# An S4 convolution block with its gradients: the Y tables of the dK reduction made beside their use, and one column tile's transform moved ahead of the K transform

## The chip, the core and the metric

The kernel runs on one core of a Trainium2 chip. The metric is device time in microseconds (us) of one execution; lower is better. Several executions are timed and the median is given. One execution was recorded by the hardware profiler.

The engines that matter here: PE (TensorE, matmuls and transposes), DVE (VectorE, elementwise), ACT (ScalarE, copies and activations), POOL (GpSimd; here almost only an issuer of DMAs) and SP (an issuer of DMAs). Each engine runs its own instructions strictly in the order in which they were written. POOL's and SP's queues, too, issue DMAs in that order, so a DMA that must wait for a buffer holds those behind it.

## The reference

Length L = 2048, width D = 512, state N = 128 per channel, FFN width F = 1792. Everything is bf16 at the boundary.

```python
x  = A_u                              # [1, 2048, 512]
xn = layernorm(x)
dt = exp(log_dt); dB = dt * B; logdA = dt * A          # complex, [512, 128]
K[d, l] = Re( sum_n C[d,n] * dB[d,n] * exp(logdA[d,n] * l) )
s  = causal_long_convolution(xn, K) + Dskip * xn       # along the sequence, FFT in the reference
g  = silu( silu(xn @ w1) @ w2 )
out = x + s * g
# outputs: out, and the vjp with grad_out for A_u, A_re, A_im, B_re, B_im, C_re, C_im,
#          log_dt, Dskip, w1, w2
```

The kernel replaces the FFT by matmuls with DFT tables. Its four "column tiles" `kt` = 0..3 are blocks of frequencies. For each it needs three spectra: U of `xn`, DS of the gradient that enters the convolution, and K. It stores them as UXd, DXd and KXd in DRAM (1 MB per tile). The products are U x K (the forward convolution y), conj(U) x DS (the gradient dK of K) and conj(K) x DS (the gradient for xn).

## The kernel before

All work is laid out by hand: `manual_schedule` keeps the order in which the Python program emits it, generators interleave several streams, and tiles come from two stacks of pools (left and right). Waits follow from the use of tiles. The program is five functions after each other.

**stage_1 (0 to 178 us)**: the FFN forward, the DFT tables, and the power tables XYd in DRAM: for each of `NB` = 4 blocks of channels a row of powers of exp(logdA), some of them times C dB.

**stage_2, table stage (178 to 302 us).** K at lag h*16 + l is a product of a high power (table X, 41 chunk positions h) and a low power times C dB (table CY, l = 0..15). `chunk_tables` (L795 to L845) builds X and CY on DVE: `prod` fills X from a few loaded powers (L819 to L823), `quads` fills the 12 missing low columns of a table (L806 to L813, 5 instructions). It also builds Y, the low powers without C dB, which only the backward pass needs; Y's low three columns serve as multipliers for CY too. `copy_tables` (ACT, L781) copies loaded base columns into Y and CY. `chunk_K` multiplies CY by X (PE); after block 3 `store_K` writes K's lags to DRAM and `load_K` reads them back in the order of the transform (K_b). In the same 15 steps per block, `gen_xt` transposes X (PE L932, ACT copy L934) and stores it as XTd, and `gen_yt` does so with Y (PE L950, ACT L951) as YTd, both on SP's queue; `fwd_classes` (L990, PE L998, ACT L999) transforms the column tiles of xn "by classes", 32 matmuls in 4 groups, leaving a radix-4 step (`rad4`, DVE L92 to L98) to finish; tile 3 of DS is done in the same way. While K travels through DRAM (the K wait), DVE does the last radix steps, the last Y quads, and the product conj(U) x DS of tile 3 (`cplx_mul`, L106 to L109) with its inverse radix step `rad_inv` into BK3.

**stage_3 (302 to 350 us), gen_kt**: four transforms of K (`fwd_eo` L1164, `add_eo` L1174 to L1179), the product with U, and the inverse radix step into BY. The rest of the XT and YT groups of block 3 is emitted between these steps.

**stage_4 (350 to 424 us)**: `DXform` transforms tiles 0, 1 and 2 of DS by the longer way, `fwd_eo` with 64 matmuls (`front`), then `mul` (add_eo and conj(U) x DS) and `inv` (into BK). Between them the y convolution runs on PE in steps `t0` of two (L1188, ps_v from BY): its result S_s (ACT L1442) is multiplied by cG = grad_out times a silu derivative of the loaded `co` (POOL loads L1323, ACT L132, DVE L1335 and L1340).

**stage_5 (424 to 575 us)** starts with the dK convolution (L1188 with BK) and, beside it on DVE, `Prod`: for each tile conj(K) x DS from KXd and DXd (loads aXl L1558) and the inverse step into BG. The DS spectrum of tile 2 is handed to Prod in SBUF. It goes on with the w2 gradient (PE L1594) and, from about 480 us, the **slab stage**: the convolution over BG (L1188), and `Slabs`, which reduces dK against the powers. Sixteen slabs (4 per block), each in three steps that a fixed grid deals out between convolution steps and halves of w2 groups (8 matmuls each):

- step 1: `P2(i, 0)`, 16 small matmuls (L1769) of a block-diagonal tile `Gbd` by the loaded XTl, with an ACT copy into Vb (L1771); `Gb(i+1)` on DVE (L1757);
- step 2: `P2(i, 1)`; `load(i+3)` (XTl on SP and POOL L1746, YTl on POOL L1747);
- step 3: `D3(i)` on DVE (L1780, L1783), Vb by YTl; then `P3(i-1)` on PE (L1798), the sum over l.

The grid for each w2 group `ft` from 4 is: one convolution step while any is left (ft up to 9), one slab step, half a group, two slab steps, half a group, two slab steps.

**stage_6 (575 to 752 us)**: the FFN backward and LayerNorm's gradient.

Of the kernel before, what the change touches and what calls it, by code (L numbers as in the profile page):

```python
# [135 lines left out]
def kernel(ctx, tc, A_u, A_A_re, A_A_im, A_B_re, A_B_im, A_C_re, A_C_im, A_log_dt, A_Dskip, B_x, B_w1, B_w2, grad_out,  # L136
# [28 lines left out]
    k.XTd = dr.tile([NB, 64 * NR, 2, P], BF16, name="XTd"); k.YTd = dr.tile([16, P, 2, 4, P], BF16, name="YTd")  # L165
# [121 lines left out]
class Setup:  # L287


    def __init__(self, k, W1, W2, pr, fs):  # L290
# [27 lines left out]
        k.num = const.tile([P, 49], I32, name="num")  # L318
# [403 lines left out]
def tables_open(k, fs):  # L722

    lo = k.left
    k.mm = lo.open("mm")
    sa = lo.open("sa")
    k.tabs, k.gt, k.gc = {}, {}, {}
    k.slot = [(sa, sa), None]
    XY = fs.tile([P, 11, 2, 64, 2], BF16, name="XYc", tag="aT")

    def more():
        k.nc.gpsimd.dma_start(XY[:].rearrange("p i c q e -> p i (c q e)"), k.XYd[:, 17:NT, 0])
# [4 lines left out]
    k.gt[0] = chunk_tables(k, 0)  # L737
    k.nt0 = 0
    k.ko = lo.open("ko"); k.xc = lo.open("xc")
    k.Kout = k.ko.tile([P, NH, P], BF16, name="Kout")  # L740


def ld_tab(k, b):

    XY = k.xc.tile([P, 11, 2, 64, 2], BF16, name="XYc", tag="XYc")
    k.nc.sync.dma_start(XY[:].rearrange("p i c q e -> p i (c q e)"), k.XYd[:, 17:NT, b])
    k.gc[b] = copy_tables(k, b, XY)
    k.gt[b] = chunk_tables(k, b)
# [13 lines left out]
def open_y(k, b):  # L762

    slot, cys = k.slot[b % 2]
    k.tabs[b]["Y"] = slot.tile([P, 2, 64, 16, 2], BF16, name="Y", tag="Y")
    k.tabs[b]["CY"] = cys.tile([P, 2, 64, 16, 2], BF16, name="CY", tag="CY")
# [13 lines left out]

def copy_tables(k, b, XY):  # L781

    Y, CY = k.tabs[b]["Y"], k.tabs[b]["CY"]

    def cp(x, o, i, n):
        k.nc.scalar.copy(out=cq(x, o), in_=XY[:, i:i + n].rearrange("p i c q e -> p (c q) i e"))
    cp(Y, slice(1, 4), 0, 3)
    yield
    cp(Y, slice(0, 16, 4), 3, 4)
    yield  # L790
    cp(CY, slice(0, 16, 4), 7, 4)
    yield


def chunk_tables(k, b):  # L795
# [6 lines left out]
    def quads(x, op0, op1):  # L802
        fl = lambda m: m.rearrange("p c q (a b) e -> p (c q) a b e", a=4)
        m1, m2 = mt("m1", 12), mt("m2", 12)
        qd = x[:].rearrange("p c q (a b) e -> p c q a b e", a=4)
        TT(out=fl(m1), in0=qd.rearrange("p c q a b e -> p (c q) a b e")[:, :, :, 0:1].to_broadcast([P, 128, 4, 3, 2]),  # L806
           in1=cq(t["Y"], slice(1, 4)).unsqueeze(2).to_broadcast([P, 128, 4, 3, 2]), op=ALU.mult)
        q4 = lambda m, c: m[:, c].rearrange("p q (a b) e -> p q a b e", a=4)
        for c in range(2):
            TT(out=q4(m2, c), in0=qd[:, c, :, :, 0:1].to_broadcast([P, 64, 4, 3, 2]), in1=t["Y"][:, 1 - c, :, 1:4].unsqueeze(2).to_broadcast([P, 64, 4, 3, 2]), op=ALU.mult)  # L810
        TT(out=qd[:, 0, :, :, 1:4], in0=q4(m1, 0), in1=q4(m1, 1), op=op0)
        i, j = (0, 1) if op1 == ALU.add else (1, 0)
        TT(out=qd[:, 1, :, :, 1:4], in0=q4(m2, i), in1=q4(m2, j), op=op1)  # L813
# [18 lines left out]
    if b == 0:  # L832
        quads(t["CY"], ALU.add, ALU.subtract)
        yield
# [6 lines left out]
    if b:  # L841
        quads(t["CY"], ALU.add, ALU.subtract)
        yield
    quads(t["Y"], ALU.subtract, ALU.add)
    yield  # L845
# [75 lines left out]
def gen_xt(k, xs, b):  # L921
# [3 lines left out]
    for n in range(11):  # L925
        ks = range(4 * n, min(4 * n + 4, 41))
        if n % 2 == 0:
            XT = xs.tile([P, 8, 2, P], BF16, name="XT", tag="XT", bufs=4)
# [9 lines left out]
        yield  # L938


def gen_yt(k, xs, i0):
    nc = k.nc
    YT = xs.tile([P, 2, 2, 4, P], BF16, name="YT", tag="XT", bufs=4)
    for i in (i0, i0 + 1):
        b, u, s, q0 = slab(i)
        Y = k.tabs[b]["Y"]
        pt = k.ps.tile([P, 2, 4, P], BF16, name="pt_yt", tag="ps")
        for c in range(2):
            for b4 in range(4):
                nc.tensor.transpose(out=pt[:, c, b4, :], in_=Y[:, c, q0 + 4 * b4:q0 + 4 * b4 + 4].rearrange("p w l e -> p (w l e)"), identity=k.ident[:])  # L950
        nc.scalar.copy(out=YT[:, i - i0], in_=pt[:])  # L951
        if i > i0:
            k.put(k.YTd[i0:i0 + 2].rearrange("i p c b n -> p i (c b n)"), YT[:].rearrange("p i c b n -> p i (c b n)"))
        yield
# [48 lines left out]
def stage_2(k):  # L1003
# [3 lines left out]
    k.tf2 = ro.open("tf2"); k.xs = ro.open("xs", 2); sb = ro.open("sb"); k.slot[1] = (sb, ro.open("cyb")); dsc = ro.open("dsc"); uw = ro.open("uw", 2)  # L1007
# [20 lines left out]
    for b in range(2):  # L1028
# [8 lines left out]
        for _ in fr:  # L1037
            tables_0(k)
    for b in range(NB):
# [3 lines left out]
        gy = [gen_yt(k, k.xs, i) for i in (4 * b, 4 * b + 2)]  # L1043
        sl = [gx] * 11 + [g for g in gy for _ in range(2)]
# [4 lines left out]
        if b == 2:  # L1049
            sl, gy2 = sl[:11], sl[11:]  # L1050
        if b:
            open_y(k, b + 1)
        fr = front(b + 2) if b < 2 else fwd_classes(k, dsc, k.DS, st["TF"], st.setdefault("D", {}))
        for j in range(15):
            if j in ((3, 9), (0, 3, 6), (0, 3))[b]:
                next(gw)
            if j in ((8, 10, 12, 14), (1, 4, 7, 10), (8, 13))[b]:
                next(fr)
            if j < 4:
                next(Tc, None)  # L1060
            if j == 0 and b < 2:
                next(k.gt[b])
# [15 lines left out]
    next(k.gt[2])  # L1078
    for g in gy2:
        next(g)  # L1080
# [8 lines left out]
    k.by = lo.open("by"); k.uxp = lo.open("uxl")  # L1089
    k.TFs1 = ld_tf(k, 1, nc.gpsimd)  # L1090
    UX = ld_ux(k, 0)
    radix(3)
    next(k.gt[3])
    sl = iter(sl)
    for n in range(8):
        next(next(sl))
# [5 lines left out]
    k.BY = k.by.tile([P, 4, 2, 4, W], BF16, name="BY", tag="B")  # L1102
    k.tn = lo.open("tn"); bk3 = lo.open("bk3")
    kq = k.kq = lo.open("kq")
    k.sel = lo.open("sel")
    k.row = k.sel.tile([DK, P], BF16, name="row")
# [6 lines left out]
    k.BK3 = rad_inv(k, bk3, "BK3", PX)  # L1113
    k.dskb = dskip_out(k)
    return gk, sl, held


def rad_inv(k, pool, tag, PX):

    B_ = pool.tile([P, 2, 4, W], BF16, name="BK", tag=tag)  # L1120
    t = k.mm.tile([P, 2, 4, W], BF16, name="r4_t", tag="cm_t2")
    rad4(k.nc, B_[:, :, 0:2], B_[:, :, 2:4], PX, t[:].rearrange("p e (c m) w -> p e c m w", c=2), True)
    return B_
# [143 lines left out]
def stage_3(k, gk, sl, held):  # L1267
# [3 lines left out]
    for n, _ in enumerate(gk, 1):  # L1271
# [4 lines left out]
        for g in (next(sl, None) for _ in range(n >= 4)):  # L1276
            if g is not None:
                next(g)
# [94 lines left out]
class DXform:  # L1373
# [7 lines left out]
    def front(self, kt):  # L1381
# [8 lines left out]
        for n, _ in enumerate(fwd_eo(k, A, lambda t: k.DS[:, t, :], TFs, TN)):  # L1390
            if n == 0 and kt < 2:
                k.TFs = ld_tf(k, kt + 1, k.nc.scalar)
            yield

    def mul(self, kt):
# [3 lines left out]
        if kt < 2:  # L1399
            nc.gpsimd.dma_start(k.DXd[kt], XD[:])  # L1400
        else:
            k.pr = Prod(k, XD)
        self.PX = cplx_mul(nc, k.mm, self.UX, XD, conj_a=True)
        if kt < 2:
            self.UX = ld_ux(k, kt + 1)

    def inv(self, kt):
        k = self.k
        k.BK.append(rad_inv(k, self.bk if kt else k.tf2, f"BK{kt}" if kt else "TFs", self.PX))
        if kt == 2:  # L1410
            k.BK.append(k.BK3)


def stage_4(k):
# [5 lines left out]
    k.bk = lo.open("bk")  # L1420
# [6 lines left out]
    for t0 in range(0, T, TS):  # L1427
# [3 lines left out]
        if t0 == 8:  # L1431
            for _ in dx.front(2):
                pass
            dx.mul(2)
# [18 lines left out]
        if t0 == 10:  # L1453
            dx.inv(2)
# [92 lines left out]
class Prod:  # L1547
# [4 lines left out]
    def __init__(self, k, XD):  # L1552
        self.k = k
        self.ld = {0: (self.get(k.kq, "A", k.KXd, 0), XD)}
# [49 lines left out]
def stage_5(k):  # L1604
# [40 lines left out]
    gs(T - 2)  # L1645
    Gt = k.Gt = k.tf2.tile([P, 16, 256], BF16, name="Gt", tag="TFs")
# [16 lines left out]
    lo.close("bk", "sel", "kq", "bk3", "tn", "uxl")  # L1663
# [52 lines left out]

class Slabs:
# [3 lines left out]
    def __init__(self, k, sw):  # L1721
# [5 lines left out]
        self.newV(0)  # L1727

# [9 lines left out]
    def load(self, i, q=None):  # L1738
        k, nc = self.k, self.k.nc
        dma = (q or nc.sync).dma_start  # L1740
        YT = self.YT[i] = self.sw.tile([P, 2, 4, P], BF16, name="YTl", tag="YT", bufs=4)
# [5 lines left out]
        nc.gpsimd.dma_start(YT[:], k.YTd[i])  # L1747
# [61 lines left out]
    def steps(self):  # L1809

        self.Gb(0)
        for i in range(16):
            self.P2(i, 0)
            if i + 1 < 16:
                self.Gb(i + 1)
            yield
            self.P2(i, 1)
            self.XT.pop(i), self.G.pop(i)
            if i + 3 < 16:
                self.load(i + 3)  # L1820
            yield
            self.D3(i)
            if i:
                self.P3(i - 1)
            if i > 1 and i % 4 == 1:
# [7 lines left out]
class Bwd:  # L1833
# [23 lines left out]
    def dh(self, n):  # L1857
# [5 lines left out]
        sd = self.fw.tile([P, 2, 512], BF16, name="sd", tag="sd")  # L1863
# [37 lines left out]
    def dx(self, tc_, dhT):  # L1901
# [3 lines left out]
        for t in range(4 * tc_, 4 * tc_ + 4):  # L1905
# [5 lines left out]
            dxn = k.fx.tile([P, D], F32, name="dxn", tag="dxn")  # L1911
            m12 = fw.tile([P, 2], F32, name="m12", tag="m12"); c12 = fw.tile([P, 2], F32, name="c12", tag="c12")
            nc.vector.scalar_tensor_tensor(out=dxn[:], in0=psx[:], scalar=1.0, in1=self.DXC[:, t, :], op0=ALU.mult, op1=ALU.add, accum_out=m12[:, 0:1])
            t1 = k.fx.tile([P, D], F32, name="ln_t1", tag="ln_t1", bufs=1)
            nc.vector.scalar_tensor_tensor(out=t1[:], in0=dxn[:], scalar=1.0, in1=k.xn[:, t, :], op0=ALU.mult, op1=ALU.mult, accum_out=m12[:, 1:2])
            nc.vector.tensor_scalar(out=c12[:], in0=m12[:], scalar1=k.rstd[:, t:t + 1], scalar2=-1.0 / D, op0=ALU.mult, op1=ALU.mult)  # L1916
            nc.scalar.activation(out=dxn[:], in_=dxn[:], func=ACT.Identity, scale=k.rstd[:, t:t + 1], bias=c12[:, 0:1])  # L1917
# [4 lines left out]
    def rest(self):  # L1922
# [7 lines left out]
        nc.vector.scalar_tensor_tensor(out=dxn[:], in0=k.xn[:, t, :], scalar=c12[:, 1:2], in1=dxn[:], op0=ALU.mult, op1=ALU.add)  # L1930
        O1 = fw.tile([P, D], BF16, name="O1", tag="O1")
# [110 lines left out]
```

## Time and profile before

| | us |
|---|---|
| three runs, median | 758.52 |
| three runs, lowest and highest | 752.28, 761.05 |
| the profiled execution, its own time | 754.35 |
| the profiled execution, its span | 752.2 |
| mean granted TensorE clock | 0.967 of full |
| PE busy | 665.2 (88%) |
| DVE busy | 619.8 (82%) |
| ACT busy | 444.4 (59%) |
| POOL busy | 124.4 (17%) |
| bytes moved by DMA | 198.86 MB, mean 264 GB/s |

All times of single instructions count from the start of the profiled span; 2 us of the execution's own time lie outside the span. An engine's busy time is summed over its instructions; PE's matmuls are pipelined, so that the recorded 0.38 us of a 512-wide matmul overlaps the next one, which starts 0.216 us later. An arrow after an idle time names what released the engine. A line number is that of the source; where a helper such as `rad4` or `cplx_mul` emits the instruction, all its callers share that line, and the name of the written tile tells them apart.

### The profile page before, as it was taken

Reading aid. Unit: us, or ns where it says so; the run is one execution under the profiler, and the core shown is the slowest. Engines: PE = TensorE matmul, PEld = TensorE weight load, DVE = VectorE, ACT = ScalarE, POOL = GpSimd, SP = SyncE. Lnnn points to the kernel's source line nnn. Section 1 sums busy time; section 2 is a strip of 40 time slices with the busy share of each in tenths; the row PEclk is TensorE's granted clock in tenths of the full one; section 3 lists DMA queues with packets and bytes.
Section 4 is the critical chain, followed back from the end, with each engine's and each line's share of the span. In section 5 each row is a group of like instructions: output and inputs, shape, how many; then the busy total and the mean of one; then the engine's idle time right before and its main releaser. Section 6 shows DMA issues by size and latency. Waiting matters only on the chain. (4 is left out here: it accounts for less than half of the span.)

```text
span 752.2 us, 13787 instructions
## 1 busy us (share of the span) xinstructions
PE 665.2 (88%) x5356; PEld 347.0 (46%) x5356; DVE 619.8 (82%) x965; ACT 444.4 (59%) x541; POOL 124.4 (17%) x192
## 2 busy tenths in 40 slices
PE   4768978798978777999999899989999999889998
PEld 2434444353646566454444344434444554444444
DVE  6899999998999798699999999654685579988810
ACT  4789888986769857375435322244566765764211
POOL 2334071021002003000012111311131000111210
PEclk9999998999989997999999999999999999999999
DMA  9647766899898969899667889798895987788591
GB/s 270 235 160 254 239 212 240 273 315 362 266 318 280 289 189 215 302 375 380 247 248 250 298 324 339 227 331 303 279 298 170 283 230 225 234 251 280 186 344 52
DMA packets 153155, 198.86 MB, mean 264 GB/s; under 512 B 29405, under 2 KB 114788, under 8 KB 147170
## 3 DMA queue, kind: packets, MB, share of 16 engines
q1 hardware_dynamic: 133314, 129.48, 54.6%
q0 software_dynamic: 11840, 54.07, 20.0%
q10 hardware_dynamic: 7936, 14.43, 5.9%
q8 instruction: 42, 0.69, 0.4%
q14 instruction: 23, 0.19, 0.1%
HBM read 112.72 MB, written 83.38 MB: 261 GB/s over the span
## 5 line engine op out<-in xcount | busy, mean ns | idle before, releaser
L607 PE MATMUL ps_h<-XNT,W 128*128 128x512 bf16 x224 | 61.1, 423 | 13.8 <-ACT hs L610 13.8
L1188 PEld LDWEIGHTS <-TIs 128*128 128x128 bf16 x384 | 37.3, 98 | 50.4 <-issue 4.4
L580 PE MATMUL ps_o<-W,aT 128*128 128x512 bf16 x224 | 54.3, 391 | 1.8 <-DVE ak L76 1.8
L1869 PE MATMUL ps_da<-DOT,W2T 128*128 128x512 bf16 x224 | 52.9, 379 | 1.5 <-ACT DOT L1849 1.1
L1908 PE MATMUL ps_dx<-W1T,dhT 128*128 128x512 bf16 x224 | 52.9, 379 | 0.0
L1870 DVE TENSOR_TENSOR dhT<-ps_da,sd 128x1024 bf16<-128x1024 f32 x28 | 34.1, 1221 | 22.0 <-ACT sd L132 16.3
L1594 PE MATMUL ps_w<-DO_all,AW 128*128 128x512 bf16 x224 | 52.0, 380 | 0.0
L1992 PE MATMUL ps_w<-dhc,xn 128*128 128x448 bf16 x256 | 49.3, 352 | 1.0 <-DMA dhc<-dhd 1.0
L1780 DVE TENSOR_TENSOR T<-Vb,YTl 128x2048 bf16<-128x2048 bf16 x16 | 19.6, 1223 | 35.9 <-ACT Vb L1771 35.6
L1164 PEld LDWEIGHTS <-TFs 128*128 128x128 bf16 x312 | 30.2, 98 | 37.4 <-issue 2.8
L934 ACT COPY XT<-pt_xt 128x1024 bf16<-128x1024 bf16 (+1 forms) x44 | 41.3, 1004 | 4.0 <-DMA XTd<-XT 3.0
L1771 ACT CAST Vb<-ps_V 128x1024 bf16<-128x1024 f32 x32 | 31.7, 1013 | 17.9 <-PE ps_V L1769 12.0
L607 PEld LDWEIGHTS <-W 128*128 128x128 bf16 x224 | 22.7, 105 | 39.4 <-issue 22.8
L1164 PE MATMUL ps_f<-K_b,TFs 128*128 128x512 bf16 x168 | 38.9, 379 | 1.7 <-DMA K_b<-Kud 1.2
L1917 ACT ACTIVATE dxn<-dxn,c,rstd 128x512 f32<-128x512 f32 x16 | 13.0, 814 | 45.0 <-DVE c L1916 45.0
L580 PEld LDWEIGHTS <-aT 128*128 128x128 bf16 x224 | 22.8, 102 | 31.2 <-issue 7.4
L1992 PEld LDWEIGHTS <-xn 128*128 128x128 bf16 x256 | 25.0, 98 | 24.9 <-DMA dhc<-dhd 1.5
L998 PE MATMUL ps_f<-xn,TFs 128*128 128x512 bf16 x128 | 33.1, 414 | 2.4 <-DMA TFs<-TFd 2.4
L1893 ACT COPY dhk<-pt_dh 128x1024 bf16<-128x1024 bf16 x28 | 28.0, 1001 | 10.2 <-PE pt_dh L1891 10.2
L1869 PEld LDWEIGHTS <-W2T 128*128 128x128 bf16 x224 | 21.6, 98 | 26.8 <-issue 2.2
L1164 PE MATMUL ps_f<-DS,TFs 128*128 128x512 bf16 x144 | 33.0, 379 | 0.7 <-ACT S_s L1442 0.7
L1594 PEld LDWEIGHTS <-AW 128*128 128x128 bf16 x224 | 20.2, 98 | 26.7 <-issue 4.7
(345 smaller groups left out, 1570.6 us busy)
## 6 DMA issues: line engine op xcount, KB each, us to landing
TIs<-TId SPq DMA_DIRECT2D x24, 512.0 KB, 6.5
XTd<-XT SPq DMA_DIRECT2D x20, 512.0 KB, 4.5
XTl<-XTd SPq DMA_DIRECT2D x15, 512.0 KB, 8.1
hTd<-hs SPq DMA_DIRECT2D x28, 256.0 KB, 3.5
akd<-ak SPq DMA_DIRECT2D x28, 256.0 KB, 3.6
UXl<-UXd POOLq DMA_DIRECT2D x7, 1024.0 KB, 7.9
dhd<-dhk SPq DMA_DIRECT2D x28, 256.0 KB, 5.3
XYd<-XYg SPq DMA_DIRECT2D x25, 256.0 KB, 4.5
```

Of the source, the lines that this page charges most:

```text
L580: nc.tensor.matmul(out=pso[:], lhsT=aT[:, ft, tt * P:(tt + 1) * P], rhs=W2[:, ft, :], start=(ft == 0), stop=(ft == FT - 1))
L607: nc.tensor.matmul(out=ps[:, j], lhsT=W1[:, dk, ft * P:(ft + 1) * P], rhs=XNT[:, dk], start=(dk == 0), stop=(dk == DK - 1))
L934: nc.scalar.copy(out=XT[:, j0:j0 + len(ks)], in_=pt[:, 0:len(ks)])
L998: nc.tensor.matmul(out=ps[:, c, :], lhsT=TFs[:, t1 + 4 * j, c, :], rhs=src[:, t1 + 4 * j, :], start=(j == 0), stop=(j == 3))
L1164: nc.tensor.matmul(out=ps[:, c, :], lhsT=tab(j), rhs=at(t1 + 4 * j), start=(n == 0), stop=(n == 4 * len(terms) - 1))
L1188: nc.tensor.matmul(out=ps[:, j, :], lhsT=TIs[:, j, 2 * kt + c, :], rhs=B[kt][:, c, (t0 + j) % 4, :], start=(kt == 0 and c == 0), stop=(kt ...
L1594: nc.tensor.matmul(out=ps[:], lhsT=A[:, t, :], rhs=k.DO[:, t, :], start=(t == 0), stop=(t == T - 1))
L1771: nc.scalar.copy(out=self.V[i][:, g2], in_=ps[:].rearrange("p b c n -> p c b n"))
L1869: nc.tensor.matmul(out=ps[:, j], lhsT=self.W2T[:, ft // 2, dk, j * P:(j + 1) * P], rhs=self.DOT[tc_][:, dk], start=(dk == 0), stop=(dk == ...
L1870: nc.vector.tensor_tensor(out=self.dhT[:, f0:f0 + 2, :], in0=ps[:], in1=sd[:], op=ALU.mult)
L1908: nc.tensor.matmul(out=psx[:], lhsT=dhT[:, ft, t % 4 * P:(t % 4 + 1) * P], rhs=self.W1T[:, ft, :], start=(ft == 0), stop=(ft == FT - 1))
L1992: nc.tensor.matmul(out=ps[:], lhsT=k.xn[:, t, dk * P:(dk + 1) * P], rhs=ch[i][:, t, :], start=(t == 0), stop=(t == T - 1))
```

## The change

**Y.** The Y tables, their transposes and YTd are no longer made in the table stage. What stays there is Yb, the low three columns (128x768) that CY's quads need. In the slab stage Y is built for half a block at a time, two slabs, numbered m = 0..7: `load_y` (two POOL loads per block) brings the seven base columns of Y from XYd; `Ybase(m)` copies them on ACT into the working tile Ys (and the low three into Yb for an even m); `Yquad(m, c)` fills the missing columns of component c with three DVE products of 128x768; `Yt(i)` transposes one slab's part with 8 PE transposes and an ACT copy into YT (two buffers), which D3 reads in the place of YTl.

```diff
+    def Yquad(self, m, c):
+        if m >= 8:
+            return
+        ...
+        for j in range(2):
+            TT(out=m4(j), in0=qd[:, j, :, :, 0:1].to_broadcast([P, 32, 4, 3, 2]),
+               in1=self.Yb[:, j ^ c, q0:q0 + 32].unsqueeze(2).to_broadcast([P, 32, 4, 3, 2]), op=ALU.mult)
+        TT(out=qd[:, c, :, :, 1:4], in0=m4(0), in1=m4(1), op=ALU.add if c else ALU.subtract)
+
+    def Yt(self, i):
+        k, nc = self.k, self.k.nc
+        pt = k.ps.tile([P, 2, 4, P], BF16, name="pt_yt", tag="ps")
+        for c in range(2):
+            for b4 in range(4):
+                q = 16 * (i % 2) + 4 * b4
+                nc.tensor.transpose(out=pt[:, c, b4, :], in_=self.Ys[:, c, q:q + 4].rearrange("p w l e -> p (w l e)"), identity=k.ident[:])
+        YT = self.YT[i] = self.sw.tile([P, 2, 4, P], BF16, name="YT", tag="YT", bufs=2)
+        nc.scalar.copy(out=YT[:], in_=pt[:])
 
     def steps(self):
         self.Gb(0)
         for i in range(16):
+            m = i // 2 + 1
             self.P2(i, 0)
             if i + 1 < 16:
                 self.Gb(i + 1)
+            if i % 2 == 0:
+                self.Yt(i)
             yield
             self.P2(i, 1)
             self.XT.pop(i), self.G.pop(i)
             if i + 3 < 16:
                 self.load(i + 3)
+            if i % 2 == 0:
+                self.Yt(i + 1)
             yield
             self.D3(i)
             if i:
                 self.P3(i - 1)
+            if i % 2 == 0:
+                self.Ybase(m)
+                if i % 4 == 0 and i < 12:
+                    load_y(k, i // 4 + 1)
+            self.Yquad(m, i % 2)
             if i > 1 and i % 4 == 1:
                 self.store(i // 4 - 1)
             yield
```

`Slabs.__init__` makes Y of pair 0 (`Ybase(0)`, `Yquad(0, 0)`, `Yquad(0, 1)`). In the table stage `quads(t["Y"], ...)`, `gen_yt` and their steps go, and the load of base columns is 7 columns in two DMAs instead of 11 in one:

```diff
-    quads(t["Y"], ALU.subtract, ALU.add)
-    yield
...
-        nc.gpsimd.dma_start(YT[:], k.YTd[i])
...
+def load_y(k, b):
+    for o, i, n in ((2048, 20, 4), (3072, 17, 3)):
+        k.nc.gpsimd.dma_start(k.yb[:, o:o + 256 * n].rearrange("p (i z) -> p i z", i=n), k.XYd[:, i:i + n, b])
```

**Tile 2 of DS.** It is transformed by classes in the table stage like tile 3 (32 matmuls), its radix step and the store DXd[2] come after `store_K`, and its product and inverse step run in place during the K wait. In stage 4 `front(2)`, `mul(2)` and `inv(2)` go, and Prod reads tile 2 of DS from DRAM, on POOL's queue ahead of the loads of `co` and `cG` for step 12:

```diff
-            if j in ((8, 10, 12, 14), (1, 4, 7, 10), (8, 13))[b]:
+            if j in ((6, 8, 10, 12, 14), (1, 4, 7, 10, 13), (2, 5, 8, 11))[b]:
                 next(fr)
...
     store_K(k)
-    next(k.gt[2])
-    for g in gy2:
-        next(g)
+    XD2 = st["D2"]["A"]
+    rad(XD2)
+    nc.gpsimd.dma_start(k.DXd[2], XD2[:])
...
     XD = st["D"]["A"]
     rad(XD)
     nc.gpsimd.dma_start(k.DXd[3], XD[:])
+    PX = cplx_mul(nc, k.mm, st[2]["A"], XD2, conj_a=True)
+    k.BK2 = XD2
+    rad_inv(k, XD2, PX)
     PX = cplx_mul(nc, k.mm, st[3]["A"], XD, conj_a=True)
...
         if t0 == 8:
-            for _ in dx.front(2):
-                pass
-            dx.mul(2)
+            k.pr = Prod(k)
...
-            dx.inv(2)
...
-        self.ld = {0: (self.get(k.kq, "A", k.KXd, 0), XD)}
+        self.ld = {0: (self.get(k.kq, "A", k.KXd, 0), self.get(k.kq, "X", k.DXd, 0))}
```

**Places.** The transform of U that stage 3 needs first is read into BY[:, 0] instead of a buffer of its own; XT has six buffers instead of four, and all XT groups of block 3 are emitted in the K wait, so that stage 3 holds none; some pools open earlier or later; in stage 6 the f32 rows `dxn` and `ln_t1` lie in one tile (`fx`) in the buffer of DS tile 2, still with two rows for `dxn`:

```diff
-            XT = xs.tile([P, 8, 2, P], BF16, name="XT", tag="XT", bufs=4)
+            XT = xs.tile([P, 8, 2, P], BF16, name="XT", tag="XT", bufs=6)
...
-    UX = ld_ux(k, 0)
+    UX = k.BY[:, 0]
+    nc.gpsimd.dma_start(UX, k.UXd[0])
...
-            dxn = k.fx.tile([P, D], F32, name="dxn", tag="dxn")
+            dxn = k.fx[:, t % 2]
```

More of the change, by code (lines that the diff above doesn't have):

```diff
@@ L832, in chunk_tables @@
     if b == 0:
-        quads(t["CY"], ALU.add, ALU.subtract)
+        quads()
         yield
@@ L937, in gen_xt @@
             k.put(k.XTd[b, P * k0:P * k1].rearrange("(k p) c n -> p k c n", p=P), XT[:, 0:k1 - k0])
[L938 to L953, printed above, removed]
         yield
```

184 lines of the change are left out of this document (103 added, 81 removed).

## The prediction

> **What bounds the kernel now.** I read the page first, then busy times by stage, then the chain of waits and the order of time inside the three places that the change touches.
>
> ```profile
> span 752.2 us, 13787 instructions
> PE 665.2 (88%) x5356; PEld 347.0 (46%) x5356; DVE 619.8 (82%) x965; ACT 444.4 (59%) x541; POOL 124.4 (17%) x192
> ```
>
> PE and DVE are both nearly full; the answer differs by stage. In the next view each row is a stretch in us, its length, then the busy time of PE, PEld, DVE, ACT and POOL, the granted clock and the DMA share.
>
> ```profile
> 178.00:240.00 62.00, 51.45 (x776) 31.83 (x778) 58.98 (x93) 42.94 (x48) 9.31 (x15) 0.92 0.92 301
> 240.00:302.00 62.00, 47.85 (x949) 37.10 (x942) 55.77 (x78) 45.95 (x53) 10.57 (x20) 0.89 0.86 234
> 302.00:350.00 48.00, 47.56 (x258) 23.13 (x258) 41.23 (x51) 24.76 (x27) 2.63 (x6) 1.00 0.95 345
> 388.00:424.00 36.00, 32.71 (x152) 14.65 (x150) 35.15 (x37) 14.81 (x16) 6.73 (x13) 1.00 0.85 300
> 424.00:480.00 56.00, 55.29 (x252) 24.22 (x252) 54.90 (x61) 15.23 (x19) 7.18 (x13) 1.00 0.82 287
> 480.00:553.00 73.00, 69.54 (x689) 31.63 (x691) 40.98 (x57) 37.05 (x43) 19.94 (x33) 1.00 0.88 295
> 553.00:576.00 23.00, 21.37 (x259) 9.81 (x252) 18.15 (x26) 13.62 (x17) 5.33 (x10) 1.00 0.75 260
> ```
>
> The table stage (178 to 302) is DVE's, with DMA close behind. From 314 to 480 DVE has hardly a gap (35.15 of 36.00, then 54.90 of 56.00). The slab stage from 480 is PE's (69.54 of 73.00): only there does DVE have room, 32.0 us, and the change moves DVE work from the first place into the last.
>
> **Table stage: Y quads out.** One Y quad group in the order of time on DVE:
>
> ```profile
> 255.97 1.09 DVE L819 TENSOR_TENSOR m<-X 128x1792 bf16<-128x1792 bf16 x1 [4.06 <-DMA X<-XYd]
> ...
> 272.44 1.75 DVE L806 TENSOR_TENSOR m<-Y 128x3072 bf16<-128x3072 bf16 x1
> 274.11 1.82 DVE L810 TENSOR_TENSOR m<-Y 128x1536 bf16<-128x1536 bf16 x2
> 275.96 1.15 DVE L811 TENSOR_TENSOR Y<-m 128x1536 bf16<-128x1536 bf16 x1
> 277.03 0.94 DVE L813 TENSOR_TENSOR Y<-m 128x1536 bf16<-128x1536 bf16 x1
> ```
>
> From 272.44 to 278.01 that is 5.5 us, and four leave. Those of blocks 0 and 1 stand ahead of the last table that K needs (CY of block 3, done at 272.4): 2 x 5.3 = 10.6 us of DVE before the K store. But the first row shows DVE waiting 4.06 us for block 3's X to load; asking sooner makes that wait longer. DMA is helped (a block's 1 MB of YTd stores and 0.26 MB of XYc go), and XTd stores still stand ahead of those loads on SP's queue. Ends: 3 us, if the longer wait eats most, and 9, if the loads come sooner by nearly as much. I take 5. PE gains 32 class matmuls for DS tile 2 (4 groups of 8, 1.73 each, 6.9 us) and loses 64 Y transposes ahead of the K store (8 groups of 0.44, 3.5): 3.4 more, and PE is idle for 24.7 us in the two rows. If PE were the bound there, the early start would fall to 1.6.
>
> **The K wait.** Between the end of CY and the first add of the K transform (314.07) DVE now does three radix passes (3 x 4.9), two complex products (2 x 7.0), two inverse passes (2 x 4.8) and the Dskip sums (1.5): 39.8 us, against 41.7 from 272.4 to 314.07. It fits by 2 us, without the old Y quads; an old wait of 5.85 us at 304.3 before the inverse of tile 3 shows that the order isn't tight by itself. Loss 0 to 2, I take 0.5. All XT(3) transposes now lie in this wait too; PE and ACT are half idle there. So 4.5 us early into stage 3 (3 to 8).
>
> **Stage 4: column tile 2 out.** DVE loses add_eo (2.4), product (7.0) and inverse (4.8), 14.2 us, at 408.83 to 425.6; PE loses 64 matmuls, 13.8 us at 393.62 to 407.43. The full 14.2 would arrive if only DVE counted. But the dK conv on PE starts after the last steps of the y conv, and these after a load:
>
> ```profile
> 412.21 0.54 POOL L1323 DMA_DIRECT2D co<-od  x1
> ...
> 422.13 1.06 ACT L132 ACTIVATE co<-co 128x1024 bf16<-128x1024 bf16 x1 [6.57 <-DMA co<-od]
> ...
> 424.15 7.07 PE L1188 MATMUL ps_v<-BK,TIs 128*128 128x512 bf16 x32 [2.74 <-ACT S_s L1442]
> ```
>
> ACT waits 6.57 us for co of step 12, and the S_s copy behind it on ACT releases PE's accumulator. POOL issues that co behind one 1 MB load of the products (aXl); after the change behind two, because the transform of tile 2, until now in SBUF, comes back from DRAM. An aXl takes 8.5 us to land (the DMA view of 376 to 428) and the row moves 300 GB/s, so a second MB is worth about 3.5; the UXl load that goes (1 MB) stood earlier in the same queue and gives part of it back. I put the start of the dK conv at 419 to 421.5 on the old clock. From it PE runs 53.4 us without a gap to 477.6; DVE's own chain would allow the end 10 us sooner. Gain 4.6 to 10, I take 6 (the PE end is the nearer); 14.2 stays as the far bound.
>
> **Slab stage: Y for two slabs at a time.** Added per slab: 8 PE transposes, 0.44 us (323.99 to 324.43 for one Y group), 7.0 in all; an ACT copy of 1.02; three DVE products of 128x768, 548 ns each by the L821 row, 1.64 us, or about 1.55 back to back; some 0.9 of ACT base copies. Gone: the YTl loads, and perhaps the 3.4 us that PE waits for XTl. Per slab DVE goes from 3.7 (D3 2.43, Gb 1.28) to 5.3, 84 us in a stage that is 87 us from the first P2 to the end. What matters is the order. The row of the waits, and one slab:
>
> ```profile
> DVE T L1780 <- ACT Vb L1771: 35.6, 11, 9.8
> ```
> ```profile
> 541.82 1.01 ACT L1771 CAST Vb<-ps_V 128x1024 bf16<-128x1024 f32 x1
> 542.86 1.23 DVE L1780 TENSOR_TENSOR T<-Vb,YTl 128x2048 bf16<-128x2048 bf16 x1 [3.12 <-ACT Vb L1771]
> 543.18 0.40 PE L1798 MATMUL ps_S<-T,Sel 128*32 128x512 bf16 x4
> 543.62 0.61 PE L1769 MATMUL ps_V<-XTl,Gbd 128*32 128x256 bf16 x16
> 544.16 1.90 PE L1594 MATMUL ps_w<-DO_all,AW 128*128 128x512 bf16 x8
> 546.00 0.34 PEld L1769 LDWEIGHTS <-Gbd 128*32 128x32 bf16 x16 [0.42 <-DVE Gbd L1757]
> ```
>
> DVE's idle time lies before D3, and the second Y quad of a pair is issued behind the D3 that ends it. The first transposes of the next pair sit on PE two calls later, with P3, P2 and the w2 matmuls queued behind them. So P2 to Yt takes V copy 1.0 + D3 2.43 + quad 1.55 + hops, about 5.1 us; PE has P3 0.44, P2 0.54 and mostly one half of w2 (1.84) to fill it, 2.8. It then waits 2 to 2.3 us in five pairs, 3.8 or more where no half falls between, nothing where a conv (3.46) does: 14 to 16 in all. In the tail without convs (D3 of slab 9 at 547.71, of 15 at 572.56, 24.85 us) DVE alone needs 6 x 3.7 + 5 x 1.55 = 30. Sum: 7.0 + 15 + some of the tail that is not the same stall, less some of the 3.4: 22. On POOL's queue eight base loads (0.54 us to issue) take the place of sixteen YTl loads, and SP's XTl loads keep their places: 0; a base load stands between XTl parts, and one that lands late would hold ACT's base copy and the V copies behind it. Lower end 12: transposes 7 and a tail that costs 5, all else covered. Upper end 30: ACT's 1.9 us more per slab in front of the V copy as well, or base columns that land late.
>
> The Trainium skill ("TensorE: Matmul & The Clock Gate", Part 4: PE-mode transpose) speaks against putting transposes here: about 275 ns each in a kernel, and they don't keep the clock gate warm. By its price the 128 would cost 35 us; eight of them in 0.44 us (55 ns each) in this trace decide against it.
>
> **Unchanged.** Stage 6 does the same work with tiles placed elsewhere, and the UX of tile 0 is read into BY with the same bytes: 0. Without two buffers for its f32 rows stage 6 would wait on LayerNorm's, but it keeps two.
>
> **Sum.** -4.5 - 6 + 22 = +11.5 on the profiled execution's own 754.35 us (span 752.2), about 765.9. The three runs' median is 758.52, 4.2 above it; I put the forecast a little above, 767.
>
> **Rivals.** *The slab stage swallows it.* DVE has 32.0 us idle in 480 to 553, room for 25 us of quads; if the scheduled fillers cover the waits, only 12 remains, and with 8 early from the tables and 10 from stage 4 the sum is -6: 748. It decides when PE's wait for Y is under 0.5 us a pair. Against it: that idle time is in front of D3, and the quads come after.
> *The early start is lost.* X loads bound the table stage (DMA share 0.92), K is stored 1 us earlier: -1 - 6 + 22 = +15: 769.
> *Slabs cost 30.* ACT or the clock: with idle gaps among transposes the clock was 0.92 and 0.89 in the first two rows, and the 91 us of PE work would grow by 10 at 0.9. Against it: 1.00 in 302:350, which has 50 transposes. The sum is 754.35 + 19.5: 774. The skill's page, same part, would make the clock its cause.
>
> **Chances.** Forecast 0.50, swallowed 0.22, early start lost 0.14, slabs 30 0.14. About 1% is what a measurement tells from none. Slower by more: 0.34 + 0.11 + 0.14 = 0.59; within 1%: 0.16 of the forecast, 0.04 and 0.03, 0.23; faster 0.18. Range 749 to 778, the swallowed case to the upper end of the costly one; the forecast's own is 760 to 774.
>
> **What would show it.** K's store near 275.5 instead of 280.6; the first add of the K transform near 309.5; the conv over BG near 469 instead of 479.6; slabs then ending near 587 instead of 575.4; a new row "PE pt_yt <- DVE Yg" of 10 to 16 us; 7 us of L950-like transposes in the slabs. Without that row, or with DVE idle still 30 us there, the slab step is wrong; with the dK conv at 410, stage 4 was too low.

## The result and the profile after

The changed kernel took 790.4 us (median of six runs, 787.0 to 793.86) against 759.4 for the kernel before: ratio 1.043, 95% interval 1.037 to 1.049. The profiled execution took 790.77 us, 36.4 more than the one before; 767 was forecast, and the range ended at 778.

```profile
span 789.0 us, 13661 instructions
PE 662.5 (84%) x5251; PEld 344.3 (44%) x5324; DVE 626.4 (79%) x997; ACT 446.6 (57%) x554; POOL 123.5 (16%) x186
...
PEclk9999979999999788999987999999989999999999
```

PE's busy time is about the same in a longer span (73 of its 5324 matmuls have no record in this trace, so its sum is a little low). The last row is the granted clock in 40 slices of the span, in tenths; it falls in four places. The kernel before has falls in the first 302 us too, but none like the two at 395 to 434 and 572 to 592:

```profile
PEclk9999998999989997999999999999999999999999
```

By stretch (length, then busy time of PE, PEld, DVE, ACT and POOL, the granted clock, the DMA share):

```profile
302.00:350.00 48.00, 41.10 (x182) 18.20 (x184) 39.13 (x48) 20.03 (x21) 2.12 (x4) 0.93 0.83 295
350.00:388.00 38.00, 36.82 (x168) 16.53 (x171) 37.66 (x34) 17.83 (x20) 3.06 (x6) 1.00 0.59 218
388.00:424.00 36.00, 21.04 (x81) 8.50 (x80) 33.29 (x47) 8.59 (x10) 8.56 (x19) 0.83 0.78 282
424.00:480.00 56.00, 53.54 (x223) 22.68 (x227) 47.87 (x44) 14.91 (x18) 7.52 (x11) 0.93 0.83 296
480.00:553.00 73.00, 66.88 (x605) 31.94 (x613) 42.48 (x67) 43.33 (x56) 13.35 (x19) 0.98 0.73 236
553.00:613.00 60.00, 45.95 (x499) 22.40 (x496) 40.37 (x63) 33.16 (x42) 8.44 (x15) 0.91 0.48 150
```

In 388:424 PE is idle for 15 of 36 us, where it was busy for 32.71 before. Milestones, read from the order of time of the traces (us from the start of the span; three kernels of the experiments below stand beside the two):

| | before | after | after, stores on SP | after, stage-4 order | the three edits |
|---|---|---|---|---|---|
| K store issued | 280.6 | 276.9 | 275.0 | 276.1 | 276.1 |
| first add of the K transform | 314.1 | 318.2 | 310.2 | 317.1 | 311.7 |
| y conv starts | 378.8 | 380.3 | 372.4 | 379.3 | 373.8 |
| dK conv starts | 424.2 | 429.2 | 422.2 | 414.9 | 408.9 |
| conv over BG starts | 477.6 | 486.5 | 477.0 | 471.3 | 467.4 |
| first P2 | 488.8 | 497.1 | 487.5 | 481.7 | 477.8 |
| last P3 | 575.0 | 611.2 | 603.1 | 598.3 | 573.3 |
| span | 752.2 | 789.0 | 779.8 | 775.4 | 749.7 |

Three stretches lost time: the K wait (store to add) 7.8 us, which turned 3.7 early into 4.1 late; from the add to the conv over BG 4.8; the slabs 27.8. Each has its own wait in the trace. The K wait, on PE, ACT, POOL and DVE:

```profile
309.32 1.89 PE L1159 MATMUL ps_f<-K_b,TFn 128*128 128x512 bf16 x4 [6.74 <-ACT TFn L1124]
...
308.20 1.06 ACT L1124 ACTIVATE TFn<-TFs 128x1024 bf16<-128x1024 bf16 x1 [11.73 <-DMA UXd<-XU]
...
297.60 0.54 POOL L1018 DMA_DIRECT2D UXd<-XU  x1
...
310.64 1.23 DVE L97 TENSOR_TENSOR BK<-r_t 128x2048 bf16<-128x2048 bf16 x1 [4.39 <-DMA DXd<-XU]
```

K is back and PE has begun, but ACT may not write TFn: its tile lies where the XU buffer was, and the store of that buffer to UXd, issued on POOL at 297.6 behind the last K_b loads and two 1 MB loads, lands only at 308.1.

The 4.8 us between the add and the conv over BG are made up of three parts: 2.6 won up to the y conv, 3.5 lost from there to the dK conv, and 3.9 lost behind the start of the dK conv. In stage 4, waits from 380 to 487 (engine, line, what it waited for: total us, times, longest):

```profile
ACT S_s L1432 <- DVE DO_all L1332: 13.9, 3, 6.0
PE ps_v L1183 <- ACT S_s L1432: 11.1, 2, 9.1
POOL co L1315 <- DVE cG L1327: 10.9, 1, 10.9
...
PE ps_v L1183 <- DMA TIs<-TId: 5.8, 2, 3.8
```

PE waits for S_s, S_s for DO_all on DVE, and DVE works on mul(1) and inv(1) from 395.9 to 410.0 ahead of it. Before, PE did front(2) in that time and went on to the y conv without a wait:

```profile
393.62 4.48 PE L1164 MATMUL ps_f<-DS,TFs 128*128 128x512 bf16 x20 [0.70 <-ACT S_s L1442]
...
407.43 13.98 PE L1188 MATMUL ps_v<-BY,TIs 128*128 128x512 bf16 x64
```

The 3.9 us behind the start of the dK conv are mostly a wait for a load of TIs and matmuls that run slower behind it: the next 16 took 5.15 us to the start of what follows, where 3.45 is usual.

```profile
434.80 1.28 PE L1183 MATMUL ps_v<-BK,TIs 128*128 128x512 bf16 x4 [2.03 <-DMA TIs<-TId]
```

The slabs:

```profile
DVE T L1815 <- ACT Vb L1806: 29.9, 11, 4.7
...
PE pt_yt L1780 <- DVE Yg L1772: 16.9, 6, 3.6
```

The row that the prediction asked for is there with 16.9 us, in six pairs.

### The profile page after: what moved, and what is told of

Its sections match the earlier page's. It is cut to its first block, busy times and chain, and to the rows that moved or that the text cites. A ratio compares the mean times of both kernels' runs of the same rounds, so it can differ in the third digit from the quotient of the medians.

```text
span 789.0 us, 13661 instructions
## 1 busy us (share of the span) xinstructions
PE 662.5 (84%) x5251; PEld 344.3 (44%) x5324; DVE 626.4 (79%) x997; ACT 446.6 (57%) x554; POOL 123.5 (16%) x186
## 5 line engine op out<-in xcount | busy, mean ns | idle before, releaser
L607 PE MATMUL ps_h<-XNT,W 128*128 128x512 bf16 x212 | 59.9, 427 | 14.5 <-ACT hs L610 13.8
L1183 PEld LDWEIGHTS <-TIs 128*128 128x128 bf16 x384 | 39.3, 103 | 69.8 <-issue 23.9
L580 PE MATMUL ps_o<-W,aT 128*128 128x512 bf16 x221 | 52.0, 380 | 2.0 <-DVE ak L76 1.9
L1183 PE MATMUL ps_v<-BY,TIs 128*128 128x512 bf16 x125 | 33.6, 431 | 15.2 <-ACT S_s L1432 11.1
L1815 DVE TENSOR_TENSOR T<-Vb,YT 128x2048 bf16<-128x2048 bf16 x16 | 19.6, 1224 | 29.9 <-ACT Vb L1806 29.9
L1159 PEld LDWEIGHTS <-TFs 128*128 128x128 bf16 x264 | 25.9, 99 | 31.7 <-issue 1.1
L1963 ACT ACTIVATE fx<-fx,c,rstd 128x512 f32<-128x512 f32 x16 | 13.0, 813 | 45.0 <-DVE c L1962 45.0
L945 PE MATMUL pt_xt<-ident_bfloat,X 128*128 128x128 bf16 x328 | 26.0, 231 | 14.0 <-ACT XT L947 10.1
L1770 DVE TENSOR_TENSOR Ym<-Yg,Yb 128x768 bf16<-128x768 bf16 x32 | 16.4, 553 | 24.0 <-ACT Yg L1758 23.9
```

The costliest lines, as they stand in the source:

```text
L580: nc.tensor.matmul(out=pso[:], lhsT=aT[:, ft, tt * P:(tt + 1) * P], rhs=W2[:, ft, :], start=(ft == 0), stop=(ft == FT - 1))
L607: nc.tensor.matmul(out=ps[:, j], lhsT=W1[:, dk, ft * P:(ft + 1) * P], rhs=XNT[:, dk], start=(dk == 0), stop=(dk == DK - 1))
L1159: nc.tensor.matmul(out=ps[:, c, :], lhsT=tab(j), rhs=at(t1 + 4 * j), start=(n == 0), stop=(n == 4 * len(terms) - 1))
L1183: nc.tensor.matmul(out=ps[:, j, :], lhsT=TIs[:, j, 2 * kt + c, :], rhs=B[kt][:, c, (t0 + j) % 4, :], start=(kt == 0 and c == 0), stop=(kt ...
```

## The experiments

Ratios are to the kernel before, which was timed again with each group of runs (medians 753.6 to 759.4). For the changed kernel itself the ratio is 1.043. Places and waits come from one trace of each kernel, and places move a little between traces of the same code: the K store lies between 274.4 and 277.6 in the ten kernels with the same table stage, and the slab span between 114.1 and 117.0 in the seven with the same slab steps.

**Stores on SP.** Only the queue of two stores in the K wait:

```diff
-    radix(3)
+    radix(3, nc.sync)
...
-    nc.gpsimd.dma_start(k.DXd[3], XD[:])
+    nc.sync.dma_start(k.DXd[3], XD[:])
```

> Changed kernel with one edit: in the K wait the stores of UXd[3] and DXd[3] go out on SP's queue, right behind its K_b loads, and no longer on POOL's behind the last K_b loads and two 1 MB loads. In the changed kernel's trace ACT waits 11.73 us for the UXd store before it can write TFn (which lies where the store reads), PE waits 6.74 us for TFn, and DVE 4.39 us for the DXd store before BK3. Theory A (place and queue: TFn and BK3 lie on memory that a late store still reads): both waits go, the first add of the K transform moves from 318.2 to about 310 to 312, and since DVE runs without a gap from there to the y conv the whole program gains 6 to 8 us: about 783. Rival B (the DMA engines are the bound in the K wait, the stores then take time from K_b): K_b lands as much later, add near 316, total within 3 us of 790.

Measured: 781.6 us, ratio 1.036 (1.032 to 1.040). The first add came at 310.22, and the gain of 8.0 us is still there at the y conv (372.36).

```profile
299.70 3.40 PE L1159 MATMUL ps_f<-K_b,TFs 128*128 128x512 bf16 x15 [2.19 <-DMA K_b<-Kud]
302.93 1.03 PE L1159 MATMUL ps_f<-K_b,TFn 128*128 128x512 bf16 x4
```

PE no longer waits for TFn (ACT still waits 5.33 us for the store, but TFn is written before PE comes to it); 2.19 us of rival B's cost (K_b later) are there too, a quarter of what is won.

**TFn's place.** The stores stay on POOL; the pool of TFn is opened first:

```diff
-    k.uxp = lo.open("uxl"); k.tn = lo.open("tn"); bk3 = lo.open("bk3")
+    k.tn = lo.open("tn"); k.uxp = lo.open("uxl"); bk3 = lo.open("bk3")
```

> Changed kernel with the pool of TFn (tn) opened ahead of the pool of the UX loads (uxl), so that TFn lies 8 KB per partition lower and the first user of the higher place is the UX load of tile 1, which is issued later; stores stay on POOL. Theory A (TFn's wait comes from the place, memory that the UXd store still reads): TFn's 11.73 us wait goes, PE's 6.74 with it; DVE still waits for DXd before BK3 (310.6), so the first add comes at about 314.5 to 316 instead of 318.2; total down 2 to 4: 786 to 788. Rival B (TFn overlaps another late reader or the store's queue alone matters): no change, 790.

Measured: 783.1 us, ratio 1.037 (1.033 to 1.041). ACT wrote TFn at 294.86 with no wait, while DVE still waited before BK3:

```profile
294.86 1.17 ACT L1124 ACTIVATE TFn<-TFs 128x1024 bf16<-128x1024 bf16 x1
...
309.04 1.23 DVE L97 TENSOR_TENSOR BK<-r_t 128x2048 bf16<-128x2048 bf16 x1 [4.19 <-DMA DXd<-XU]
```

The add came at 312.92. Place alone removes the wait, without any change to the store; the two runs together show that the loss in the K wait is a tile laid on a buffer that a late store still reads. The total came 3 us below the range that was expected.

**The stage-4 order.**

```diff
-    dx.inv(0)
     for t0 in range(0, T, TS):
-        if t0 == 4:
-            dx.mul(1)
-            dx.inv(1)
-        if t0 == 8:
-            k.pr = Prod(k)
+        if t0 == 6:
+            dx.inv(0)
+        if t0 == 8:
+            dx.mul(1)
+        if t0 == 10:
+            dx.inv(1)
...
             y.load(t0 + 4)
+        if t0 == 8:
+            k.pr = Prod(k)
```

> Changed kernel with stage 4 in another order: inv(0) is emitted at step 6 of the y conv, mul(1) at 8, inv(1) at 10 (were: before step 0, at 4, at 4), and the two Prod loads come after the co and cG loads of step 12. Theory A (with front(2) gone PE has nothing left to do while DVE, in order, works off inv(0), mul(1), inv(1) ahead of the cG and DO_all products that free S_s): PE's waits of 9.06, 2.07 and 3.77 us go, the dK conv starts near 415 instead of 429.15, conv(0) near 472 instead of 486.5, total about 777. Rival B (the loads of co and TIs decide, 300 GB/s in this stage): dK conv no earlier than 425, total 786 to 790.

Measured: 776.8 us, ratio 1.029 (1.026 to 1.032); dK conv at 414.94, conv over BG at 471.25, both within 1 us of theory A.

```profile
403.71 7.08 PE L1183 MATMUL ps_v<-BY,TIs 128*128 128x512 bf16 x32 [0.96 <-DMA TIs<-TId]
414.94 1.46 PE L1183 MATMUL ps_v<-BK,TIs 128*128 128x512 bf16 x3 [4.15 <-DMA TIs<-TId]
```

The waits for S_s are gone; what is left are waits for the TIs loads, which rival B named. The run moves Prod's loads as well; the next run does that alone, and no run has the new order with these loads left where they were.

**Prod's loads alone.** The same move of `k.pr = Prod(k)` without the new order on DVE. It tests the reason that the prediction gave.

> Changed kernel with only the Prod loads of step 8 moved behind the co and cG loads of step 12 on POOL's queue; DVE's order is kept. The prediction's reason for a late dK conv was co of step 12 behind 2 MB. If that is what holds stage 4, co of step 12 lands some 7 us sooner than 423.8 and the dK conv starts near 422: total about 783. If DVE's order is (theory A of the run before), POOL is still held until 411 by the co buffer that DVE frees at 410, and the gain is 0 to 3 us: 787 to 790; it may lose as much if Prod's own first product now waits for its 2 MB.

Measured: 788.3 us, ratio 1.044 (1.041 to 1.047): no gain in the total. The dK conv started at 426.19, 3.0 us sooner, of which 1.7 were there at the y conv; it did not come to 422. POOL was held until 409.3 and PE as long as before:

```profile
410.97 6.55 PE L1183 MATMUL ps_v<-BY,TIs 128*128 128x512 bf16 x16 [9.06 <-ACT S_s L1430]
```

**The second quad ahead of D3.**

```diff
             self.P2(i, 0)
+            if i % 2:
+                self.Yquad(m, 1)
...
-            self.Yquad(m, i % 2)
+            if i % 2 == 0:
+                self.Yquad(m, 0)
```

> Changed kernel with one call moved in the slab steps: the second Y quad of a pair, Yquad(m, 1), is emitted behind P2(i, 0) of the odd slab, ahead of its D3, instead of behind that D3. Theory A (the in-order path V copy, D3, quad, transposes stalls PE 16.9 us, and the clock falls after each stall): the row PE pt_yt <- DVE Yg falls from 16.9 to under 4 us, the granted clock in the slab tail goes from 0.91 to near 1.0, total down by 14 to 20: 770 to 776. Rival B (DVE is full there, 5.3 us a slab, and D3 is now later by the quad): the wait turns up at P3 or P2 instead, total down by less than 6: 784 to 790.

Measured: 771.0 us, ratio 1.021 (1.018 to 1.024); first P2 to last P3 95.9 us in the place of 114.1 (95.4 and 97.1 in the two other kernels with this edit below). The waits for Yg are gone from PE's list; 5.7 us of waits for Gbd, which the quad now precedes, are the part in which rival B is right. Two stretches of the changed kernel's slabs, and then of this one:

```profile
497.00:562.00 65.00, 56.43 (x582) 27.68 (x591) 41.72 (x66) 40.72 (x52) 8.28 (x14) 0.97 0.71 231
562.00:612.00 50.00, 38.56 (x433) 18.66 (x438) 36.11 (x55) 28.12 (x37) 7.45 (x13) 0.90 0.49 152
```
```profile
495.00:560.00 65.00, 61.77 (x677) 30.01 (x677) 49.37 (x77) 46.01 (x60) 10.98 (x18) 1.00 0.78 255
560.00:592.00 32.00, 28.20 (x353) 14.01 (x352) 28.12 (x43) 22.20 (x30) 4.80 (x9) 1.00 0.56 181
```

The clock is back at 1.00, and in the tail DVE is busy for 28.12 and PE for 28.20 of 32.00 us: both are nearly full there.

**No quads, and no Y at all.** Two runs that leave out work to find its price. The first leaves out the Y quads (it returns at once from Yquad); the second also leaves out base copies, transposes and loads, and D3 multiplies by a constant tile.

> Changed kernel without the Y quads on DVE; base copies, the 128 transposes and the YT copies stay. It leaves out the 12 missing columns of Y. Theory A (the wait for the quads is the larger part, the transposes and copies 7 to 9 us): slab span 114 - 17 to 21 = 93 to 97, total about 770. Rival B (transposes and ACT copies are the larger part): slab span over 102, total over 778.

Measured: 768.8 us, slab span 91.4, 1.6 under theory A's interval.

> Changed kernel without any Y work in the slab stage: no base loads and copies, no quads, no transposes; D3 multiplies by a constant tile. It leaves out Y. It prices the Y part of the slab stage (predicted 22, 12 to 30; the traces say 27.5 from the first P2 to the end, 114.1 against 86.6). Theory A (all of that is Y's): total 790 - 27 to 30 = 760 to 763, slab span at or below 86.6. Rival B (part of it is clock or loads that have nothing to do with Y): slab span still over 92.

Measured: 757.2 us, 3 below theory A's 760, ratio 1.002 (0.999 to 1.006), slab span 82.3. So Y costs 114.1 - 82.3 = 31.8 us in the slabs: 9.1 for transposes, base and YT copies (91.4 - 82.3), 22.7 for the quads, of which 18.2 (114.1 - 95.9) go with the order alone and 4.5 don't. Without Y the stage is 4.0 us shorter than the one before; its YTl loads are gone, but no run tests these alone.

**The Y part alone**, tile 2 of DS again in stage 4:

> The Y part of the change alone: tile 2 of DS is transformed in stage 4 by front(2), mul(2), inv(2) as in the kernel before, its inverse going to the d2 buffer; Y as in the changed kernel. Theory A (moving tile 2 out of stage 4 brings nothing there, since PE only waits instead, and it fills the K wait on DVE): total 786 to 791, the dK conv within 2 us of the changed kernel's 429.15. Rival B (moving it brings the 6 us that were predicted, and the loss ahead of the slabs is all from TFn's place): total 796 or more.

Measured: 785.1 us, ratio 1.039 (1.033 to 1.044). The total is 1 us below theory A's interval; its interval overlaps that of the whole change, so moving tile 2 brought nothing, and at the conv over BG it cost 7.5 us (478.96 against 486.49). Of these, 3.7 are there at the K store (273.24 against 276.90) and 4.5 at the y conv (375.88 against 380.34), ahead of stage 4. On the place of the dK conv theory A missed: 423.04, not within 2 us of 429.15.

**The Y part alone, in the later stage-4 order:**

> The Y part alone with tile 2 of DS in stage 4, but in the later order: inv(0) at step 6, mul(1) and front(2) at 8, inv(1) and mul(2) at 10. It asks whether the 14 us that the stage-4 order gave in the whole change are due to the order alone. Theory A (with front(2) to fill PE and 14.2 us more on DVE, DVE is the bound whatever the order): dK conv at 421 to 425 as without the order (423.0), total 783 to 788. Rival B (the order alone gives it): dK conv at 413 to 416, total near 775.

Measured: 790.2 us, ratio 1.045 (1.041 to 1.050). The total is 2 us above theory A's interval. The dK conv starts at 420.78 and then waits 9.67 us for the inverse of tile 2, which comes last in this order and too late with 14.2 us more on DVE:

```profile
420.78 1.03 PE L1178 MATMUL ps_v<-BK,TIs 128*128 128x512 bf16 x4
431.48 7.63 PE L1178 MATMUL ps_v<-BK,TIs 128*128 128x512 bf16 x28 [9.67 <-DVE BK L97]
```

In this form the order alone is worth nothing. It pays when tile 2 is out of stage 4, and taking tile 2 out pays with the order: neither alone.

**The Y part alone with the quad ahead of D3:**

> The Y part of the change alone (tile 2 of DS in stage 4 as before), with the second quad ahead of D3. The Y part alone took 785; the quad's place was worth 18 us of slab span in the whole change. If that is a matter of the slab stage alone: 785 - 18 = 767, slab span 96. If the early start of the slabs or the load of POOL's queue has a share in it: over 771.

Measured: 763.8 us, ratio 1.011 (1.008 to 1.015), slab span 97.1. That is 21 us less than the Y part alone, where 18 were expected: the quad's place is a matter of the slab stage alone.

**The three edits together.**

> The three edits together: stores of UXd[3] and DXd[3] on SP, the stage-4 order, the second quad ahead of D3. If the three causes are independent and each as large as expected (7, 13, 17): 790 - 37 = 753, a little below the kernel before. If the second and third hide each other (DVE or DMA bound in the end): 765 or more.

Measured: 750.2 us, ratio 0.994 (0.991 to 0.997). The ratios of the single edits lose 0.007, 0.014 and 0.022 from 1.043, 0.043 in sum; together they lose 0.049. Within the intervals the causes add up. This version beats the kernel before by 0.6%: the conv over BG starts 10.2 us sooner, and 9.2 of that are paid back by a slab span of 95.4 against 86.3.

**The quad behind Gb.** As the last, but with `Yquad(m, 1)` behind `Gb(i + 1)`:

> The stores on SP, the stage-4 order, and the second Y quad behind Gb(i+1) of the odd slab instead of ahead of it. With the quad ahead of Gb, PE waited 5.2 us in the slabs for Gbd, 1.3 to 1.8 us at a time in the tail. Theory A (P2 of the next slab waits for Gb, and the quad can wait 1.3 us more since D3's V copy isn't there yet): slab span from 95.4 to 90 to 93, total 746 to 748, 1% below the kernel before. Rival B (DVE is full in the tail, 30.8 of 34 us, so the order inside a slab doesn't matter): slab span 95 and total 750 again.

Measured: 750.8 us, ratio 0.993 (0.991 to 0.996), slab span 94.5. This is rival B: the waits for Gbd are replaced by 3.8 us of waits for Yg, and DVE is busy for 30.21 of the tail's 34 us. Between these two orders inside a slab there is nothing left to win.

## Why the prediction was wrong

The side was right, the size was not: +11.5 us against +36.4. The slab term alone gave the side; the two terms that were forecast as gains ahead of it both came out as losses. By its own terms:

**Table stage, -5.** The K store came 3.7 us sooner in this trace (3 to 9 was given), and 3.0 to 6.2 in the ten kernels with the same table stage. This step held. In the three kernels without the class transform of tile 2 there the store came 6.2 to 8.4 us early, so that transform takes some 2 to 3 us back, as the prediction's 3.4 us more on PE would have it.

**K wait, a loss of 0.5.** The step that failed first. DVE's sum was right: it had nothing open at 314.6 but the add itself, after its 4.39 us wait. The prediction counted DVE's work against the time and costed the moves of buffers at nothing ("Unchanged", with "the same bytes: 0"). With d2 a further 8 KB lie on the right of SBUF, TFn comes to lie on the XU buffer, and the store of that buffer is now on the path: 11.73 us on ACT, 6.74 on PE. Both edits that take it away (the queue, the place) bring the add to 310.2 and 312.9, 3.9 and 1.2 us early; the forecast was 309.5. The old wait of 5.85 us before BK3, which the prediction quoted as slack, was most likely a wait of this kind and a hint: the trace before names no releaser for it, but its UXd store took 9.3 us from its issue to landing, to 310.1, and BK3 was written from 310.19 on.

```profile
300.76 0.54 POOL L1021 DMA_DIRECT2D UXd<-XU  x1 [0.72 <-DMA K_b<-Kud]
...
310.19 1.22 DVE L97 TENSOR_TENSOR BK<-r_t 128x2048 bf16<-128x2048 bf16 x1 [5.85 <-issue]
```

**Stage 4, -6.** Wrong in sign: +4.8 between the add and the conv over BG. The prediction gave `co` of step 12 behind 2 MB as what holds the dK conv; moving those 2 MB away gained nothing. What holds it is DVE's order: inv(0), mul(1) and inv(1) come ahead of the products that free S_s, and with S_s PE's accumulators and POOL's `co` buffers. Before, front(2) gave PE 13.8 us of work just there; to take this filler from an engine that then waits bought nothing. The gain was there to be had: with the order changed (and Prod's loads moved) the dK conv starts 14.2 us sooner. The prediction also let PE run 53.4 us without a gap from the dK conv to the conv over BG; it took 57.3, with the wait for TIs in it. (Its 479.6 for that conv in the kernel before is the second piece; the first matmul is at 477.6.) After the 9.06 us wait the next 16 matmuls took 6.42 us, where 3.63 is usual:

```profile
412.67 6.42 PE L1183 MATMUL ps_v<-BY,TIs 128*128 128x512 bf16 x16 [9.06 <-ACT S_s L1432]
```

**Slabs, +22.** The mechanism and its place were as told (the wait for Yg between the two halves of a pair's transposes, six times), and moving one call took 18.2 us away. The size was low: +27.8 by span, 31.8 for Y's work less 4.0 for the loads that go. The waits were 16.9 us where 14 to 16 stood, transposes and copies 9.1 where the transposes stood with 7.0. What is left of the quads' 22.7 us behind these waits is 5.8. The clock, which the prediction had only as a rival, can make this up, but no run holds the clock fixed. The matmuls after some of the waits ran at a lower clock: after the one of 3.64 us the w2 group took 2.83 us to the next instruction's start, where 1.82 is usual:

```profile
571.24 0.40 PE L1780 MATMUL pt_yt<-ident_bfloat,Yg 128*128 128x128 bf16 x4 [3.64 <-DVE Yg L1772]
571.69 2.90 PE L1583 MATMUL ps_w<-DO_all,AW 128*128 128x512 bf16 x7
574.52 1.03 PE L1804 MATMUL ps_V<-XTl,Gbd 128*32 128x256 bf16 x16
```

(One of the eight has no record.) Short stretches behind the six waits (2.32, 1.97, 2.50, 3.64, 3.20 and 3.29 us, in this order) show the granted clock, the first number after the busy times:

```profile
524.00:529.00 5.00, 3.89 (x45) 1.95 (x46) 2.34 (x5) 2.75 (x4) 0.50 (x1) 1.00 0.19 40
541.00:544.00 3.00, 2.78 (x28) 1.64 (x22) 1.75 (x3) 2.98 (x4) 0.52 (x1) 0.54 0.68 203
558.00:562.00 4.00, 3.95 (x38) 2.02 (x38) 0.08 (x1) 2.03 (x3) 0.50 (x1) 1.00 0.12 18
573.00:576.00 3.00, 3.00 (x28) 1.21 (x26) 0.00 (x0) 0.40 (x1) 0.14 (x1) 0.60 0.38 130
585.00:588.00 3.00, 2.19 (x27) 1.48 (x28) 1.92 (x4) 1.55 (x2) 0.30 (x1) 0.61 0.04 16
601.00:604.00 3.00, 3.00 (x29) 1.30 (x28) 0.00 (x0) 0.92 (x3) 0.00 (x0) 0.72 0.00 0
```

The three waits over 3 us lowered it, and one of the three from 1.97 to 2.50 did. By their starts in the order of time, the matmuls behind these four waits took 1.5 to 1.6 us each longer than the same groups elsewhere in the slabs, some 6 us in all (an estimate). The Trainium skill ("TensorE: Matmul & The Clock Gate", Part 1: The HAM clock gate) says that a free-running window of about 3.4 us without work halves TensorE's clock; the trace agrees for the waits of 9.06 us (0.50 from 414 to 418) and 3.64 us; those of 3.20 and 3.29 us are a little shorter than that rule asks for, and the 1.97 us wait is much shorter. Around this last one, between the last w2 matmul and the next convolution, PE had only transposes and the small P2 matmuls for 4.7 us, and no run here tells whether those count. They are not needed for it: the 2.03 us wait for TIs at 434.80, with 512-wide matmuls at their usual pace right before it, lowered the clock as well (0.68 from 434 to 438). Transposes among matmuls don't lower the clock here by themselves: in the run without quads, with all 128 of them and no such waits, it is 1.00 over the 92 us of the slabs.

**Sum.** 8.6 us are lost on the K wait (-4.5 forecast, +4.1 found), 10.8 on stage 4 and 5.8 on the slabs: 25.2 in sum, where 24.9 lie between the forecast and the result. The lower end of the range, "the slabs swallow it", never was near; the costly rival (774) named the clock, but kept the gain in the other two places. Of the signs that were asked for, the K store, the Yg row (16.9 us, where 10 to 16 were asked) and the transposes came; the add, the conv over BG and the end of the slabs came 9, 17 and 24 us later than told.

## What to carry to other kernels

Before counting a removed piece of work as a gain, ask what each other engine did meanwhile: if it was filler in front of another engine's wait, the gain may come only with a new order of the work that makes it wait, as here. A change of buffers is a change of waits: list for each tile that moves which late store still reads its new place. In an in-order pipeline, produce the next stage's operand ahead of the instruction that waits, not behind it: one call moved was worth 18 us here.

## What was not expected of the hardware

Some PE waits cost more than their length: after 9.06 us of waiting, 16 matmuls took 2.8 us more, after 3.64 us a group of 8 took 1.0 more. The price varies: after the same 9.06 us in the traces of the quad ahead of D3 and of Prod's loads alone, the 16 took 5.20 and 6.55 us. A 1 MB store issued at 297.6, with the DMA engines busy for 0.98 of the time until 308.1, took 10.5 us to land.

In the three-edit version the stretch from the dK conv to the conv over BG takes 58.5 us against 53.4 before. Its trace shows where the 5 us lie: the first 16 matmuls, behind a 4.41 us wait for TIs, took 5.1 us instead of 3.6, and then PE waits 3.33 us for S_s, which ACT could copy only behind `co`, and for that load ACT had waited 7.64 us.

```profile
408.89 1.89 PE L1183 MATMUL ps_v<-BK,TIs 128*128 128x512 bf16 x4 [4.41 <-DMA TIs<-TId]
...
417.36 1.02 PE L1183 MATMUL ps_v<-BK,TIs 128*128 128x512 bf16 x4 [3.33 <-ACT S_s L1432]
```

So the load of `co`, which the prediction took for what holds stage 4, is on the path once DVE's order no longer is. What remains open is what these loads cost in all: no run took the waits for `co` and TIs away.
